# Sums of two quads in half-height products, with the last keys of all values between and behind them

## The chip, the cores and the metric

The kernel runs on one core of one Trainium2 chip. A core has five engines with queues of their own: TensorE (PE: matrix products, with its weight loads shown apart as PEld), VectorE (DVE), ScalarE (ACT), GpSimd (POOL) and SyncE (SP), which here only starts transfers. Products land in PSUM, eight banks of 128 partitions by 512 float32 numbers. The metric is the device time of one execution in microseconds (us), less is better; each number given for it is the median of several runs.

## What is computed

Cosine attention over 8 batches of 12 heads, 448 positions, 64 numbers a head, then a two-layer block with a leaky ReLU over all 3584 tokens.

```python
q_n = q / (np.linalg.norm(q, axis=-1, keepdims=True) + 1e-06)
k_n = k / (np.linalg.norm(k, axis=-1, keepdims=True) + 1e-06)
scores = np.matmul(q_n, k_n.transpose(0, 1, 3, 2)) / tau
attn = np.exp(scores - np.max(scores, axis=-1, keepdims=True))
attn = attn / (np.sum(attn, axis=-1, keepdims=True) + 1e-09)
x = np.matmul(attn, v)            # tokens x (12 heads * 64) = 3584 x 768
h = x @ w_in                      # 768 -> 2048
out = np.maximum(0.01 * h, h) @ w_out   # 2048 -> 768
```

The scores are bounded by 1/tau = 10, so the kernel takes the exponentials without the maximum.

## The kernel before

**Units.** A batch has 12 heads, that is six pairs (a *slot* s) and three quads of four heads (index j, three to a batch, `NQ = 3`). The 448 keys of a head are three tiles of 128 (`ki` = 0, 1, 2) and 64 *last keys*. Exponentials of scores lie in `pe[s]` (128 key rows, three tiles, two heads, 448 queries) and, for the last keys, in `pr[j]`: 128 rows, of which one half of 64 belongs to two heads of the quad and the other half to the other two. `rem_half(j, g)` says which half has head g of quad j; it changes over from one quad to the next. The values of the last keys lie likewise in `vrb`, with the other half of the rows zero, so that a product over all 128 rows takes only the right ones.

**Products of an attend.** For each quad the kernel needs the sums of the exponentials (weights: 32 columns of ones, so that each sum stands on 32 partitions) and, for the even and for the odd columns of v (`e` = 0, 1), the products with the values (32 columns each). One PSUM bank holds four strips of 32 partitions, one for each head. So a product here has 32 columns and goes to one strip: `strip_products` (L314) runs over key tiles and heads, four strips after each other; those over 128 rows are called `128*32` in the profile. `rem_products` (L301) does the last keys alone, over 64 rows (`64*32`), for two quads at once, whose heads use opposite halves of the rows.

**Order of an attend.** `attend_two` (L670) takes the first two quads of a batch: it deals banks (a pair for the sums, two pairs for the values), runs the last keys of sums and values by `rem_products`, then the sums of both quads with the reciprocals behind each (`totals`, `reciprocals`: ACT takes Ln of the bank at L339 and Exp of its negative at L340 into a tile `rb`), then the values of each quad (`products`) and their scaling by `rb` (`scale`, L361: DVE multiplies a PSUM bank by `rb` into `xT`, the transposed tokens). `attend` (L659) then takes the third quad by itself: four tiles of sums (the last through `ones_rem`, ones with half of the rows zero), four tiles of each half of the values. The first batch uses `attend` in another place, which does not change; seven batches go through `attend_batch` (L688).

**What stands around it.** After an attend, `firsts` runs the first layer for a chunk of tokens (L384: 16 blocks, each of six products over six slices of `xT`, the slices of quad j being 2j and 2j+1; the first three blocks are begun with four slices each). `visit` then runs the second layer of the chunk (L459, in halves of 64 rows), with key tiles of the next batch (L280 scores, L292 exponentials on ACT) dealt between. In both, `norm(s)` prepares later slots: `roots` (ACT, L200 and L201), `normalise` (DVE, L217, L218, L222), a transposing transfer on SP (L254), loads on SP, and a cast and squares on POOL.

**Order and banks.** The schedule is by hand: each engine runs its instructions in the order of the program text. `banks` deals the PSUM bank, or pair of banks, that was dealt or given back longest ago and isn't kept; a bank dealt with a name is kept until `given_back`. `behind` puts an empty instruction on an engine that waits for another one: on PE it is used where the other half of the rows goes on adding to the same bank.

Of the kernel before, what the change touches and what calls it, by code (L numbers as in the profile page):

```python
# [11 lines left out]
ALU = mybir.AluOpType  # L12
# [4 lines left out]
def kernel(  # L17
# [10 lines left out]
    nc = tc.nc  # L28
    B, H, S, D = q.shape
# [9 lines left out]
    NQ = NPAIR // 2  # L39
# [15 lines left out]
    qtp = ctx.enter_context(tc.tile_pool(name="qt", bufs=7))  # L55
    pep = ctx.enter_context(tc.tile_pool(name="pe", bufs=6))
    prp = ctx.enter_context(tc.tile_pool(name="pr", bufs=3))
    rbp = ctx.enter_context(tc.tile_pool(name="rb", bufs=2))
    xtp = ctx.enter_context(tc.tile_pool(name="xt", bufs=2))
    htp = ctx.enter_context(tc.tile_pool(name="ht", bufs=1))  # L60
    osp = ctx.enter_context(tc.tile_pool(name="os", bufs=3))
# [13 lines left out]
    def banks(count, keep=None, which=None):  # L75
        lo, hi = (0, 8) if not deals["apart"] else (0, 4) if count == 2 else (4, 8)
        x = which if which is not None else min(
            (i for i in range(lo, hi, count) if not set(range(i, i + count)) & set(sum(kept.values(), []))),
            key=lambda i: max(age[i : i + count]),
        )  # L80
        deals["n"] += 1
        age[x : x + count] = [deals["n"]] * count
        if keep:
            kept[keep] = list(range(x, x + count))
        return ps[:, x] if count == 1 else ps[:, x : x + count]

    def given_back(keep):
        deals["n"] += 1
        for i in kept.pop(keep):
            age[i] = deals["n"]  # L90
# [46 lines left out]
    def load_qk(s):  # L137
        if s >= NSLOT:
            return
        b, h0 = s // NPAIR, 2 * (s % NPAIR)  # L140
        both = raw_sb[:, s % NPAIR]
        nc.sync.dma_start(out=both[:, :, 0:3], in_=main(q, b, h0, 2))
        nc.sync.dma_start(out=both[:, :, 4:7], in_=main(k, b, h0, 2))
        for i, x in enumerate((q, k)):
            nc.sync.dma_start(
                out=both[64 * i : 64 * i + 64, :, 3],
                in_=x[b, h0 : h0 + 2, MAIN:S].rearrange("h p d -> p h d"),
            )
        raw[s] = (both[:, :, 0:4], both[:, :, 4:7])
# [3 lines left out]
    vb, vrb = {}, []  # L153
# [32 lines left out]
    def sums(s, parts=(0, 1)):  # L186
        if s >= NSLOT:
            return
        if s not in ss:
            ss[s] = smp.tile([128, 14], F32, name="ss")  # L190
        for i in parts:
            o = ss[s][:, 0:8] if i == 0 else ss[s][:, 8:14]
            nc.vector.tensor_reduce(  # L193
                o.rearrange("p (h t) -> p h t", h=2), sqs[s][i], axis=AX.X, op=ALU.add
            )
# [7 lines left out]
    qn, scalings = {}, {}  # L203

    def behind(eng, ins, why):

        tc.add_manual_dep(
            eng.nop().ins, ins.ins.name,
            mybir.DependencyInfo(mybir.DependencyClass.Sync, mybir.DependencyReason.DATA),
            reason=why,  # L210
        )
# [51 lines left out]
    pe, pr = {}, {}  # L263
# [30 lines left out]
    xT = {}  # L294

    rbs = {}

    def rem_half(j, g):
        return g // 2 ^ j % NQ % 2

    def rem_products(two, xs, weights):  # L301


        for g in range(4):
            for j, x in zip(two, xs):
                rows = slice(64 * rem_half(j, g), 64 * rem_half(j, g) + 64)
                nc.tensor.matmul(  # L307
                    out=x[32 * g : 32 * g + 32, :S],
                    lhsT=weights(j, g, rows),
                    rhs=pr[j][rows, g % 2, :],  # L310
                    start=True, stop=False,
                )

    def strip_products(j, x, weights, rem):  # L314

        begun = rem is None
        for ki in range(3 if begun else 4):
            for g in range(4):
                s, a = 2 * j + g // 2, g % 2
                nc.tensor.matmul(  # L320
                    out=x[32 * g : 32 * g + 32, :S],
                    lhsT=weights(g, ki) if ki < 3 else rem(g),
                    rhs=pe[s][:, ki, a, :] if ki < 3 else pr[j][:, a, :],
                    start=(ki == 0 and not begun), stop=(ki == (2 if begun else 3)),
                )

    sms = {}

    def totals(j, sm=None):
        rem = None if sm is not None else lambda g: ones_rem[:, rem_half(j, g)]  # L330
        sms[j] = banks(1) if sm is None else sm
        strip_products(j, sms[j], lambda g, ki: ones, rem)
        if sm is not None:
            reciprocals(j)

    def reciprocals(j):
        sm = sms.pop(j)
        rb = rbp.tile([128, S], F32, name="rb")
        nc.scalar.activation(rb, sm[:, :S], func=AF.Ln)  # L339
        nc.scalar.activation(rb, rb, func=AF.Exp, scale=-1.0)  # L340
        rbs[j] = rb

    pos = {}

    def products(j, e, po=None, begun=False):
        b, jj = divmod(j, NQ)
        if po is None:
            po = banks(1, (j, e))
        pos[j, e] = po
        vm = vb[j].rearrange("p h t (d e) -> p h t e d", e=2)  # L350
        vr = vrb[b % 2].rearrange("p j g (d e) -> p j g e d", e=2)
        strip_products(
            j, po, lambda g, ki: vm[:, g, ki, e], None if begun else lambda g: vr[:, jj, g, e]
        )

    def scale(j, e):
        b, jj = divmod(j, NQ)
        m, half = divmod(b, 2)
        if m not in xT:
            xT[m] = xtp.tile([128, KT, 2 * S], BF16, name="xT")  # L360
        scalings[j, e] = nc.vector.tensor_tensor(  # L361
            xT[m][:, 2 * jj + e, half * S : (half + 1) * S], pos.pop((j, e))[:, :S], rbs[j],
            op=ALU.mult,
        )
        if (j, e) in kept:
            given_back((j, e))

# [121 lines left out]
    ones = cpool.tile([128, 32], BF16, name="ones")  # L489
# [120 lines left out]
    roots(4)  # L610
    reciprocals(0)
    products(0, 0)

    scores(3, (0,))
    products(0, 1)
    scores(3, (1,))
    scaled(3)
# [4 lines left out]
    scores(3, (3,))  # L622
    fill(1)
    scale(0, 0)

    scores(4, (0,))
    fill(2)
    scores(4, (1,))
    totals(1)
    scaled(4)  # L630
    scale(0, 1)
    scores(4, (2,))
    transposes(5)
    reciprocals(1)
    products(1, 0)

    def begin(m, kts):
# [8 lines left out]
    for e in range(2):  # L646
        scale(1, e)
# [11 lines left out]
    def attend(j, behind=()):  # L659
        totals(j)  # L660
        reciprocals(j)
        po = banks(2)
        for e in range(2):
            products(j, e, po[:, e])
        for fn in behind:
            fn()
        for e in range(2):
            scale(j, e)

    def attend_two(j):  # L670
        two = (j, j + 1)
        sm = banks(2)
        po = [banks(2) for e in range(2)]
        vr = vrb[j // NQ % 2].rearrange("p j g (d e) -> p j g e d", e=2)
        rem_products(two, [sm[:, i] for i in range(2)], lambda j, g, rows: ones[rows])
        for e in range(2):
            rem_products(
                two, [po[e][:, i] for i in range(2)], lambda j, g, rows, e=e: vr[rows, j % NQ, g, e]
            )
        for i, j in enumerate(two):  # L680
            totals(j, sm[:, i])
        for i, j in enumerate(two):
            for e in range(2):
                products(j, e, po[e][:, i], True)
            for e in range(2):
                scale(j, e)

    def attend_batch(b):  # L688
        if b == 1:
            load_qk(14)  # L690
            load_qk(15)
            sums(12)
        attend_two(b * NQ)
        if b == 1:
            norm(12)
        attend(b * NQ + 2)


    def norm(s, transposed=True):
        if s >= NSLOT:  # L700
            return
        roots(s)
        normalise(s)
        if transposed:
            transposes(s)
        for x in (12, 13) if s == 11 else (s + 4,) if s > 11 else ():
            load_qk(x)
        ahead = {7: (), 8: (), 9: (10, 11), 10: (), 11: (12, 13)}.get(s, (s + 2,))
        if ahead:
            hold(qn[s][:, 6, 0, 0:1])  # L710
        for x in ahead:
            squares(x)
# [61 lines left out]
    for b in range(B):  # L774
# [16 lines left out]
        else:  # L791
# [3 lines left out]
            wide if b == 0 else four_late if b == 1 else three if tokens == 3 else four,  # L795
        )
        attend_batch(b + 1)
        for j in range((b + 2) * NQ, (b + 3) * NQ):
            load_v(j)
# [59 lines left out]
```

## Time and profile before

| what | us |
|---|---|
| runs of the kernel (median of 3; from, to) | 406.82 (406.67, 406.88) |
| the profiled execution, its own time | 406.75 |
| its span, first to last instruction | 404.9 |

| group of the profile | count | busy us | mean ns |
|---|---|---|---|
| L384, first layer | 760 | 147.4 | 352 |
| L459, second layer in halves of the rows | 1536 | 144.0 | 323 |
| L320, values, key tiles of 128 rows | 576 | 32.0 | 353 |
| L320, sums, key tiles of 128 rows | 288 | 16.7 | 354 |
| L320, last keys of values over 128 rows, half zeros | 80 | 7.3 | 352 |
| L320, last keys of sums over 128 rows, half zeros | 40 | 3.6 | 352 |
| L307, last keys of values over 64 rows | 112 | 4.0 | 350 |
| L307, last keys of sums over 64 rows | 56 | 2.7 | 360 |
| L361 on DVE, scaling | 48 | 27.7 | 619 |

The mean is the length of one instruction from its start to its modelled end. Products in different parts of the array overlap, so the busy time of a group is not count times mean, and the step from one to the next is shorter than the length. The share of PE is given by the union of its instructions. The granted clock of PE was 1.0 in the profiled execution.

### The profile page before, as it was taken

How to read it: one execution, taken by the hardware profiler on the slowest of the kernel's cores; microseconds unless marked ns; L12 is line 12 of the kernel's file. 1: busy time of each engine (PE TensorE's matmuls, PEld its weight loads, DVE VectorE, ACT ScalarE, POOL GpSimd, SP SyncE). 2: the span in 40 equal slices, each digit the busy share in tenths (PEclk: the TensorE clock that was granted, in tenths of full speed). 3: DMA queues.
4: the chain of work that ended last, by engine and by line, in shares of the span. 5: the costliest groups of instructions: out<-in, count | busy, mean ns of one | idle time of the engine just before them, and what ended most of it. 6: DMA issues, size and time to landing. Idle time of an engine off the chain costs nothing.

```text
span 404.9 us, 10159 instructions
## 1 busy us (share of the span) xinstructions
PE 397.6 (98%) x4086; PEld 225.4 (56%) x4096; DVE 188.1 (46%) x403; ACT 264.9 (65%) x458; POOL 140.1 (35%) x213
## 2 busy tenths in 40 slices
PE   8899999999999999999999999999999999999996
PEld 3335655444555555544886555544687555544564
DVE  6987723684655624454552626256361721130021
ACT  4997799556875689655876569745786559844200
POOL 4995533464344513343142513155122500000000
PEclk9999999999999999999999999999999999999999
DMA  7999999797789827576396844685386821110033
GB/s 188 249 226 244 214 186 219 181 183 179 157 190 153 148 62 180 117 129 170 76 181 141 126 117 120 157 117 138 90 174 120 95 45 40 40 41 2 0 78 79
DMA packets 100735, 54.21 MB, mean 134 GB/s; under 512 B 69424, under 2 KB 95440, under 8 KB 100688
## 3 DMA queue, kind: packets, MB, share of 16 engines
q1 hardware_dynamic: 76400, 40.13, 42.7%
q0 software_dynamic: 23440, 12.92, 23.5%
q8 instruction: 32, 0.52, 0.6%
q10 hardware_dynamic: 848, 0.52, 0.5%
q14 instruction: 15, 0.12, 0.1%
HBM read 45.61 MB, written 11.01 MB: 140 GB/s over the span
## 4 chain that ended last, share of the span: by engine, by line
PE 96%; ACT 1%; DVE 1%; issue 0%
PE ps L384 36%; PE ps L459 31%; PE ps L320 11%; PE ps L280 8%; PE ps L421 5%; PE ps L505 2%; PE ps L307 1%; ACT pe L292 1%; PE ps L236 1%; DVE qkT L261 0%; DVE qn L222 0%; ACT qkT L548 0%; ACT rb L340 0%; DVE warm L488 0%; DVE ss L193 0%
## 5 line engine op out<-in xcount | busy, mean ns | idle before, releaser
L384 PE MATMUL ps<-xT,w_in_sb 128*128 128x384 bf16 (+1 forms) x760 | 147.4, 352 | 0.4
L459 PE MATMUL ps<-w_out_sb,hT 64*128 64x384 bf16 x1536 | 144.0, 323 | 0.0
L292 ACT ACTIVATE pe<-ps 128x896 bf16<-128x896 f32 x144 | 124.4, 917 | 16.7 <-PE ps L280 14.9
L384 PEld LDWEIGHTS <-w_in_sb 128*128 128x128 bf16 x768 | 74.1, 98 | 71.5 <-issue 3.7
L391 ACT ACTIVATE hT<-ps 128x384 bf16<-128x384 f32 (+1 forms) x128 | 67.3, 543 | 67.2 <-PE ps L384 66.7
L459 PEld LDWEIGHTS <-hT 64*128 64x128 bf16 x1536 | 84.4, 94 | 44.7 <-PE ps L459 4.2
L182 POOL TENSOR_TENSOR sq<-raw_sb 128x512 f32<-128x512 f32 x90 | 82.7, 940 | 13.4 <-DMA raw_sb<-in_k_dram 12.6
L222 DVE TENSOR_TENSOR qn<-raw_sb,r 128x512 bf16<-128x512 f32 x96 | 56.8, 634 | 1.7
L280 PE MATMUL ps<-qkT 64*128 64x448 bf16 (+1 forms) x384 | 54.8, 353 | 1.6 <-DVE qkT L261 0.8
L193 DVE TENSOR_REDUCE ss<-sq 128x6 f32<-128x384 f32 (+1 forms) x95 | 54.5, 610 | 2.6 <-POOL sq L182 2.3
L471 DVE COPY osb<-ps 128x384 f32<-128x384 f32 x41 | 21.2, 553 | 69.7 <-PE ps L459 38.8
L514 POOL CAST seen<-qn 128x1 f32<-128x1 bf16 x44 | 8.2, 187 | 123.8 <-DVE qn L222 123.6
L217 DVE TENSOR_SCALAR ss<-ss 128x14 f32<-128x14 f32 x48 | 10.0, 209 | 73.9 <-ACT ss L201 73.8
L361 DVE TENSOR_TENSOR xT<-ps,rb 128x448 bf16<-128x448 f32 x48 | 27.7, 619 | 24.3 <-ACT rb L340 24.1
L160 POOL DMA_DIRECT2D v_b<-in_v_dram x24 | 18.6, 777 | 39.9 <-PE ps L320 39.9
L320 PE MATMUL ps<-pe,v_b 128*32 128x448 bf16 x576 | 32.0, 353 | 0.0
L280 PEld LDWEIGHTS <-qkT 64*128 64x128 bf16 (+1 forms) x384 | 17.8, 97 | 17.9 <-issue 6.6
L339 ACT ACTIVATE rb<-ps 128x448 f32<-128x448 f32 x24 | 12.9, 538 | 15.3 <-PE ps L320 14.3
L320 PEld LDWEIGHTS <-v_b 128*32 128x32 bf16 x576 | 15.1, 97 | 12.0 <-issue 0.6
L427 DVE COPY osb<-ps 128x384 f32<-128x384 f32 (+1 forms) x9 | 4.6, 513 | 36.6 <-issue 22.6
L421 PE MATMUL ps<-w_out_sb,hT 128*128 128x384 bf16 (+1 forms) x144 | 21.0, 308 | 0.0
L292 ACT ACTIVATE pr<-ps 128x896 bf16<-128x896 f32 x24 | 20.7, 923 | 0.2 <-PE ps L280 0.2
(52 smaller groups left out, 188.1 us busy)
## 6 DMA issues: line engine op xcount, KB each, us to landing
raw_sb<-in_q_dram SPq DMA_DIRECT2D x46, 192.0 KB, 3.3
raw_sb<-in_k_dram SPq DMA_DIRECT2D x44, 192.0 KB, 3.5
out_dram<-osb SPq DMA_DIRECT2D x30, 192.0 KB, 3.1
v_b<-in_v_dram POOLq DMA_DIRECT2D x24, 192.0 KB, 4.8
out_dram<-osb SPq DMA_DIRECT2D x12, 384.0 KB, 2.7
w_out_sb<-in_moe_w_out_dram POOLq DMA_DIRECT2D x4, 768.0 KB, 16.3
w_in_sb<-in_moe_w_in_dram POOLq DMA_DIRECT2D x3, 512.0 KB, 8.5
w_in_sb<-in_moe_w_in_dram POOLq DMA_DIRECT2D x2, 768.0 KB, 13.1
```

Of the source, the lines that this page charges most:

```text
L182: eng.tensor_tensor(sq, x, x, op=ALU.mult)
L193: nc.vector.tensor_reduce(o.rearrange("p (h t) -> p h t", h=2), sqs[s][i], axis=AX.X, op=ALU.add)
L222: scalings[s] = nc.vector.tensor_tensor(qn[s][:, lo:hi], x.rearrange("p h t d -> p t h d"), r[:, r0 : r0 + 2 * nt].rearrange("p (h t) -> p ...
L280: nc.tensor.matmul(out=out[:, a, :S], lhsT=x[rows, c0:c1], rhs=x[rows, 0:S], start=True, stop=True,)
L292: nc.scalar.activation(out=dst, in_=sc[:, :, :S], func=AF.Exp, scale=inv_tau)
L320: nc.tensor.matmul(out=x[32 * g : 32 * g + 32, :S], lhsT=weights(g, ki) if ki < 3 else rem(g), rhs=pe[s][:, ki, a, :] if ki < 3 else pr[j] ...
L361: scalings[j, e] = nc.vector.tensor_tensor(xT[m][:, 2 * jj + e, half * S : (half + 1) * S], pos.pop((j, e))[:, :S], rbs[j], op=ALU.mult,)
L384: nc.tensor.matmul(out=pm[:, :n], lhsT=w_in_sb[:, kt, m * 128 : (m + 1) * 128], rhs=xT[c // 2][:, kt, c0 : c0 + n], start=(kt == 0), stop= ...
L391: nc.scalar.activation(out=hT[c][:, m, :n], in_=pms.pop((c, m))[:, :n], func=AF.Prelu, alpha=0.01)
L421: nc.tensor.matmul(out=po2[:, :n], lhsT=hT[c][:, m, ts * 128 : (ts + 1) * 128], rhs=w_out_sb[:, m, lo : lo + n], start=(m == 0), stop=(m = ...
L459: done[p][i] = nc.tensor.matmul(out=pos2[p][:, i, :HALF], lhsT=hT[c][rows, m, ts * 128 : (ts + 1) * 128], rhs=w_out_sb[rows, m, half * HAL ...
L471: copy(out=osb[c, ts][:, half * HALF : (half + 1) * HALF], in_=po2[:, i, :HALF])
```

## The change

The two functions `attend_two` and `attend` give way, in the seven batches of `attend_batch`, to one, `attend_all`. It issues ten turns of eight `64*32` products (four strips times two halves of the rows). In them the lower half of the rows adds up the first quad's sums while the upper half adds up the second quad's; then each half does last keys of the four values of these quads (two turns); then each goes on with the other quad's sums; the tenth turn is the last keys of the third quad's values. For the two halves of the third quad's last keys to fill all eight places of that turn, its odd values stand with their pairs of heads changed over (strip c holds head c ^ 2), and the scaling puts them back: in two parts of 64 partitions, each read from the other half of the bank. Before a half goes on to the quad that the other half had begun, PE waits for the other half's last product there (`behind`, twice in an attend). Then come the first quad's even values, the third quad's sum, and the other values. Eight banks are dealt at once, six of them kept by name; there is a third `rb` buffer. In the second batch, `norm(12)` stands ahead of the attend instead of between its two parts.

```diff
-    rbp = ctx.enter_context(tc.tile_pool(name="rb", bufs=2))
+    rbp = ctx.enter_context(tc.tile_pool(name="rb", bufs=3))
...
-    def strip_products(j, x, weights, rem):
+    def strip_products(j, x, weights, rem, over=0):
...
-            for g in range(4):
+            for c in range(4):
+                g = c ^ over
                 s, a = 2 * j + g // 2, g % 2
                 nc.tensor.matmul(
-                    out=x[32 * g : 32 * g + 32, :S],
+                    out=x[32 * c : 32 * c + 32, :S],
...
-    def scale(j, e):
+    def scale(j, e, over=False):
...
-        scalings[j, e] = nc.vector.tensor_tensor(
-            xT[m][:, 2 * jj + e, half * S : (half + 1) * S], pos.pop((j, e))[:, :S], rbs[j],
-            op=ALU.mult,
-        )
+        po = pos.pop((j, e))
+        for lo, hi in ((0, 64), (64, 128)) if over else ((0, 128),):
+            p0 = lo ^ 64 if over else lo
+            scalings[j, e] = nc.vector.tensor_tensor(
+                xT[m][lo:hi, 2 * jj + e, half * S : (half + 1) * S],
+                po[p0 : p0 + hi - lo, :S], rbs[j][lo:hi], op=ALU.mult,
+            )
...
+    def attend_all(b):
+        j0 = b * NQ
+        sm = [banks(1) for i in range(2)]
+        po = {}
+        vr = vrb[b % 2].rearrange("p j g (d e) -> p j g e d", e=2)
+
+        def head(u, c):
+            return c ^ 2 if u == (2, 1) else c
+
+        def last_keys(u, v, c, h):
+            return u if rem_half(j0 + u[0], head(u, c)) == h else v
+
+        places = {}
+        for c in range(4):
+            for h in range(2):
+                x = [(h, None, ki) for ki in range(3)]
+                y = [(h ^ 1, None, ki) for ki in range(3)]
+                for z in (x, y):
+                    if rem_half(j0 + z[0][0], c) == h:
+                        z.append((z[0][0], None, 3))
+                mid = [last_keys((0, e), (1, e), c, h) + (3,) for e in range(2)]
+                places[c, h] = x + mid + y + [last_keys((2, 0), (2, 1), c, h) + (3,)]
+        seen, begun = {}, set()
+        for n in range(10):
+            turn = [(c, h) + places[c, h][n] for c in range(4) for h in range(2)]
+            waits = {}
+            for c, h, jj, e, ki in turn:
+                if e is None and (jj, c, h ^ 1) in seen and (jj, c, h) not in seen:
+                    waits[jj] = max(waits.get(jj, (-1,)), seen[jj, c, h ^ 1], key=lambda y: y[0])
+            for _, ins in waits.values():
+                behind(nc.tensor, ins, "the other rows' products in this bank")
+            for c, h, jj, e, ki in turn:
+                if e is not None and (jj, e) not in po:
+                    po[jj, e] = banks(1, (j0 + jj, e))
+            for i, (c, h, jj, e, ki) in enumerate(turn):
+                j, g = j0 + jj, head((jj, e), c)
+                rows = slice(64 * h, 64 * h + 64)
+                ins = nc.tensor.matmul(
+                    out=(sm[jj] if e is None else po[jj, e])[32 * c : 32 * c + 32, :S],
+                    lhsT=ones[rows] if e is None else vr[rows, jj, g, e],
+                    rhs=(pr[j] if ki == 3 else pe[2 * j + g // 2][:, ki])[rows, g % 2, :],
+                    start=(jj, e, c) not in begun, stop=e is None and h != jj and places[c, h][n + 1][1] is not None,
+                )
+                begun.add((jj, e, c))
+                if e is None:
+                    seen[jj, c, h] = (8 * n + i, ins)
+        for jj in range(2):
+            sms[j0 + jj] = sm[jj]
+            reciprocals(j0 + jj)
+
+        def values(jj, e):
+            products(j0 + jj, e, po[jj, e], True, head((jj, e), 0))
+            scale(j0 + jj, e, (jj, e) == (2, 1))
+
+        values(0, 0)
+        totals(j0 + 2)
+        reciprocals(j0 + 2)
+        for jj, e in ((0, 1), (1, 0), (1, 1), (2, 0), (2, 1)):
+            values(jj, e)
+
     def attend_batch(b):
         if b == 1:
             load_qk(14)
             load_qk(15)
             sums(12)
-        attend_two(b * NQ)
-        if b == 1:
             norm(12)
-        attend(b * NQ + 2)
+        attend_all(b)
```

More of the change, by code (lines that the diff above doesn't have):

```diff
@@ L343, with products @@
     pos = {}
-    def products(j, e, po=None, begun=False):
+    def products(j, e, po=None, begun=False, over=0):
         b, jj = divmod(j, NQ)
@@ L352, in products @@
         strip_products(
-            j, po, lambda g, ki: vm[:, g, ki, e], None if begun else lambda g: vr[:, jj, g, e]
+            j, po, lambda g, ki: vm[:, g, ki, e], None if begun else lambda g: vr[:, jj, g, e],
+            over,
         )
-    def scale(j, e):
+    def scale(j, e, over=False):
         b, jj = divmod(j, NQ)
@@ L668, in attend @@
             scale(j, e)
[L670 to L686, printed above, removed]
+    def attend_all(b):
[17 more added lines that the diff above has]
+                places[c, h] = x + mid + y + [last_keys((2, 0), (2, 1), c, h) + (3,)]
+        assert all(len(x) == 10 for x in places.values())
+        seen, begun = {}, set()
[33 more added lines that the diff above has]
+            values(jj, e)
```

## The prediction

> **What bounds the kernel now.** I read the page first: busy shares, then the chain that ended last.
>
> ```profile
> span 404.9 us, 10159 instructions
> PE 397.6 (98%) x4086; PEld 225.4 (56%) x4096; DVE 188.1 (46%) x403; ACT 264.9 (65%) x458; POOL 140.1 (35%) x213
> ...
> PE 96%; ACT 1%; DVE 1%; issue 0%
> ```
>
> TensorE (PE) is busy 98% of the span and is 96% of the chain; every other engine is at 65% or less. So a change pays or costs what it does to PE's own stream, as long as nobody makes PE wait. The list of who PE waited for confirms this: five entries, 3.2 us in all, none at the lines that the change touches, and asked for the stretch from 70 us on it is empty. PE has no slack there to hide work in either.
>
> The second view is the timeline of one attend (the stretch that turns the exponentials of one batch into sums and products), the one that begins at 216.74:
>
> ```profile
> 216.74 0.38 PE L307 MATMUL ps<-pr,ones 64*32 64x448 bf16 x8
> ...
> 216.94 0.56 PE L307 MATMUL ps<-pr,v_rem 64*32 64x448 bf16 x16
> ...
> 217.43 1.32 PE L320 MATMUL ps<-pe,ones 128*32 128x448 bf16 x24
> ...
> 218.57 2.44 PE L320 MATMUL ps<-pe,v_b 128*32 128x448 bf16 x48
> ...
> 220.84 0.74 PE L320 MATMUL ps<-pe,ones 128*32 128x448 bf16 x12
> 221.41 0.36 PE L320 MATMUL ps<-pr,ones_rem 128*32 128x448 bf16 x4
> ...
> 223.22 0.99 PE L384 MATMUL ps<-xT,w_in_sb 128*128 128x384 bf16 x5
> ```
>
> Columns: start, length, engine, line, operation, tiles, shape, count. A `128*32` product fills a quarter of the array's columns, so four run side by side; a `64*32` one fills an eighth, so eight do. I call one such set a turn. The 48 products of v_b, 12 turns, run from 218.57 to 220.84: 2.27 / 12 = **0.189 us a turn**. A narrow window gives the third turn of eight by itself:
>
> ```profile
> 217.12 0.37 PE L307 MATMUL ps<-pr,v_rem 64*32 64x448 bf16 x8
> ```
>
> So turns of eight step 216.74, 216.94, 217.12: 0.20 for the first, about 0.19 for the next, and then 0.31 to the first `128*32` product (217.43), since the shape changes. A turn of eight costs what a turn of four does and holds twice the products. The attend is 33 turns and lasts 6.48 us to the first L384. Taken by the same bounds, the seven attends last 6.57, 6.50 and five times 6.48.
>
> **The change part by part.**
>
> *Turns.* Before: 3 turns of eight (last keys of two quads' sums and values), then in fours: 6 for these quads' sums, 12 for their values, 4 for the third quad's sum, 8 for its values (2 of them on last keys, half of whose rows are zeros). After: the sums of two quads in halves are 2 x 4 x 3 x 2 = 48 products plus 8 on last keys, the values' last keys 6 x 4 = 24: 80 products, 10 turns of eight; then 4 turns for the third sum and 6 x 3 = 18 for values. 32 turns. PE issues 24 products and 24 weight loads more per attend, but in one turn less: **-0.189 us**, seven times: -1.32. There are as many changes of shape as before (0.31 into `128*32`, and the one into L384), so these cancel.
>
> *Two waits of PE on itself*, ahead of the sixth and the seventh turn of eight (n = 5 and n = 6), since the second half of the rows may add to a sum only when the first is out. Each waits for the last product of the turn three before. By the steps above that product starts 0.02 into its turn and lasts 0.36, so it ends 0.38 in, while the waiting turn is due at 3 x 0.19 = 0.57: the result is there in time. What is left is that the turn's weights aren't loaded ahead. The nearest row is the same wait behind two turns of L280:
>
> ```profile
> 119.18 0.35 PE L280 MATMUL ps<-qkT 64*128 64x448 bf16 x2
> 119.36 0.33 PE L459 MATMUL ps<-w_out_sb,hT 64*128 64x384 bf16 x2
> ```
>
> The weight loader shows 0.21 us idle there (released by PE), yet the step 119.18 to 119.36 is an ordinary 0.19. Lower bound: 0. Upper bound: a change of shape, where nothing is loaded ahead, 0.31 - 0.19 = 0.12. I take 0.02: there the 0.19 runs from the last product issued, and in a turn of eight the last is issued 0.02 after the first. 14 waits: +0.28 (0 to 1.7). Queued behind each wait are the remaining turns of PE alone.
>
> *First two attends.* They are 0.09 and 0.02 longer than the others. In the first, the second turn of L307 lasts 0.65 instead of 0.56 because a bank is still being copied out by DVE:
>
> ```profile
> 69.71 0.56 DVE L471 COPY osb<-ps 128x384 f32<-128x384 f32 x1 [5.47 <-PE ps L459]
> ...
> 70.05 0.65 PE L307 MATMUL ps<-pr,v_rem 64*32 64x448 bf16 x16
> ```
>
> The changed order asks for value banks only from the fourth turn on (some 0.58 in, 70.4, after the copy's end at 70.27). -0.11 for both; bounds -0.11 and 0.
>
> *The third sum's bank.* All eight banks are now taken, so the third sum reuses the first sum's, and waits for ACT's Ln of it. This Ln can start when the ninth turn's products end: 0.20 + 7 x 0.19 + 2 x 0.02 = 1.57 for the turn's start, 0.02 + 0.36 for its last product, 0.05 of signalling (L339 in the old order starts 0.05 after the product it needs) = 2.00. It takes 0.54 (218.23 in the timeline), so it ends at 2.54, some 2.6 with the signal back. The third sum is due after ten turns, the change of shape and three value turns: 1.76 + 0.31 + 0.20 + 0.19 + 0.19 = 2.65. Covered by 0.05 only. I take 0; the upper bound is 0.1 an attend (0.7 in all), if signals are slower, or where ACT is late, as in the first attend: roots(12) now stand ahead of the Ln (L200, L201, 0.29 + 0.21) and follow a reduction that ends at 71.33, so they end near 71.9, against 69.85 + 2.00 = 71.85.
>
> *Scalings.* The reciprocals come 0.5 us later than before (the Ln at 2.00 instead of 218.23 - 216.74 = 1.49). DVE then does six scalings at 0.54 each, and the last one in two halves of 64 rows, each as long as a whole one because the length is the 448 columns (618 ns median at L361): +0.62 us of DVE per attend. From 3.2, paced by the products, the two halves end near 7.7 after the start. L384 needs them for its sixth slice: it starts at 6.33, and twelve products of 0.163 (0.216 in the wider chunks) precede the fifth slice: 8.4 at the earliest. Hidden by 0.7 us, and what runs next on DVE (normalise, needed in the following visit) is later by as much. Cost 0; without cover, the whole 0.62 would show.
>
> *norm(12) moved* ahead of the second batch's attend: its roots (ACT), normalise (0.17 + 0.24 + 1.16 on DVE), one transposing DMA and one load on SP, the tiny cast and the squares on POOL. The two loads queued on SP ahead of it stay ahead. DVE's first scaling there moves from about 3.2 to 3.75 and has caught up by the third quad, since that one waits for products. 0. A third `rb` buffer only removes a wait of ACT on DVE.
>
> **Sum.** -1.32 + 0.28 - 0.11 = -1.15 us. Against the profiled execution (span 404.9, its time 406.75, so 1.85 around it): 405.60; it lay 0.07 below the median of 406.82, so against the median 405.67, say **405.7**.
>
> A rule bears on the sum. The Trainium skill (TensorE: Matmul & The Clock Gate, "Wait — 56ns, not 53.3ns?") has a floor of about 25 ns between starts of matmuls, however small, so that eight would need 200 ns, an estimate from that page; by it the ten turns would lose part of the gain (second rival). The trace disagrees so far: eight starts lie within 0.02 us, and the third turn follows at 0.19. The same source's TensorEngine Tiling (Array Packing), "Gotcha 1: PSUM Pressure", forbids two row halves the same bank at the same time; the turns of L307 already do this on different strips without a longer step.
>
> **The rivals.**
> 1. *The third sum waits for ACT* by 0.1 in each attend. For: cover is 0.05. Against: ACT is idle 0.9 us before its first Ln in the attend. 405.7 + 0.7 = 406.4.
> 2. *Turns of eight settle at 0.20.* For: the first step is 0.20. Against: that is also the first step after a change of shape in fours. Eight later steps x 0.011 x 7 = 0.62: 406.3.
> 3. *Each PE wait empties the array* and costs 0.10 instead of 0.02: 14 x 0.08 = 1.1: 406.8, no change. Against: the row at 119.36.
> 4. *Slower:* eight weight loads a turn stay hidden for three turns but not for ten, because they must be issued between products. It decides in turns 4 to 10. The gain of an attend, 0.189 - 0.04 + 0.016 = 0.165, is gone at 0.02 per step over eight steps. If one load (0.09, `64*32` loads at L307) stood open in each: 8 x 0.09 x 7 = 5.0: 410.7. For: only three turns in a row were ever seen. Against: the third showed no trace of it.
>
> That it does something else than it says I leave aside: the counts of products follow from the code.
>
> **How the numbers follow.** A difference under 0.2% (0.81 us) can't be told from none here. The forecast, with its own range of 405.3 (both waits free) to 406.0, has 0.67: faster. Rivals 1, 2 and 3 have 0.11, 0.07 and 0.05: within 0.2%. Rival 4 has 0.10: slower. So faster 0.67, same 0.23, slower 0.10. The range goes from 405.3 to 406.6, which takes in rivals 1 and 2.
>
> **What would show it.** Right: an attend of 6.3 us to its first L384; ten steps of about 0.19 at the new product line; PE's wait list without an entry for L320 on ACT or DVE. Wrong: a step over 0.22 at the two waits, a gap before the third sum's first product, L384 waiting for DVE L361, or steps of 0.20 and more through the turns of eight.

## The result, and the profile after

| | before | changed |
|---|---|---|
| median of 6 runs each, us | 406.85 | 405.43 |
| ratio, 95% interval | | 0.9963 (0.9951 to 0.9976) |
| profiled execution: its time, its span | 406.75, 404.9 | 405.48, 403.7 |

The changed kernel is faster: 1.42 us between the medians, 0.37% by the ratio, and no run of one kernel reaches into the runs of the other. The page's first lines and its chain look as before, a little shorter (columns: engine, busy time, share of the span, instructions; then shares of the chain by engine):

```profile
span 403.7 us, 10501 instructions
PE 396.3 (98%) x4254; PEld 224.7 (56%) x4264; DVE 194.5 (48%) x410; ACT 264.3 (65%) x458; POOL 139.5 (35%) x213
...
PE 96%; ACT 2%; DVE 1%; issue 0%
```

There are 168 products more on PE (24 in each of seven attends), yet PE is busy for less time. DVE has 6.4 us more, 4.3 of it the seven second halves of the last scalings, and PE does not wait for it: its list of waits has the same five entries as before, 3.2 us in all, and none of them lies behind 70 us. The same attend as before, in the timeline of the changed kernel:

```profile
216.25 0.76 PE L719 MATMUL ps<-pe,ones 64*32 64x448 bf16 x24
...
217.22 0.91 PE L719 MATMUL ps<-pe,ones 64*32 64x448 bf16 x24
...
217.97 0.37 PE L719 MATMUL ps<-pr,v_rem 64*32 64x448 bf16 x8
...
218.27 0.75 PE L321 MATMUL ps<-pe,v_b 128*32 128x448 bf16 x12
...
218.85 0.74 PE L321 MATMUL ps<-pe,ones 128*32 128x448 bf16 x12
...
222.55 1.64 PE L389 MATMUL ps<-xT,w_in_sb 128*128 128x384 bf16 x9
```

The tenth turn of eight starts at 217.97. Nine steps lie between 216.25 and that: 1.72, that is 0.20 and eight times 0.19. The attend ends at 222.55: 6.29 us. Its busy time by attend, from the view of windows (length, busy time of PE and count, then PEld):

```profile
70.04:76.33 6.29, 6.29 (x172) 3.34 (x169) 5.60 (x12) 4.74 (x10) 2.05 (x4) 1.00 0.63 189
122.28:128.58 6.29, 6.29 (x172) 3.39 (x169) 3.11 (x6) 4.67 (x10) 1.50 (x3) 1.00 0.74 148
164.09:170.38 6.29, 6.29 (x170) 3.35 (x169) 3.32 (x6) 4.03 (x9) 0.91 (x2) 1.00 0.20 75
```

All seven are 6.29 to 6.30 (starts to the nanosecond: 6.293 to 6.296), against 6.571, 6.503 and five times 6.48 before. The differences add up to 1.43 us. The stretches between the attends are the same within 0.001, and the tail too (45.39). What keeps the span's difference at 1.24 is the start: the first attend begins 0.19 later in this execution. In the other profiled kernels below it began anywhere from 69.78 to 70.31 (but where work was added at the start), so that is scatter ahead of the attends, not part of the change.

### The profile page after: what moved, and what is told of

The parts are those of the page before. It is cut to its first block, busy times and chain, and to the rows that moved or that the text cites. A ratio compares the mean times of both kernels' runs of the same rounds, so it can differ in the third digit from the quotient of the medians.

```text
span 403.7 us, 10501 instructions
## 1 busy us (share of the span) xinstructions
PE 396.3 (98%) x4254; PEld 224.7 (56%) x4264; DVE 194.5 (48%) x410; ACT 264.3 (65%) x458; POOL 139.5 (35%) x213
## 4 chain that ended last, share of the span: by engine, by line
PE 96%; ACT 2%; DVE 1%; issue 0%
PE ps L389 36%; PE ps L464 31%; PE ps L321 9%; PE ps L280 8%; PE ps L426 5%; PE ps L719 3%; PE ps L510 2%; ACT pe L292 1%; PE ps L236 1%; DVE qkT L261 0%; ACT qkT L553 0%; ACT pr L292 0%; ACT rb L341 0%; DVE warm L493 0%; ACT rb L340 0%
## 5 line engine op out<-in xcount | busy, mean ns | idle before, releaser
L222 DVE TENSOR_TENSOR qn<-raw_sb,r 128x512 bf16<-128x512 f32 x96 | 55.7, 621 | 1.7
L217 DVE TENSOR_SCALAR ss<-ss 128x14 f32<-128x14 f32 x48 | 11.5, 239 | 70.6 <-ACT ss L201 70.3
L366 DVE TENSOR_TENSOR xT<-ps,rb 128x448 bf16<-128x448 f32 (+1 forms) x55 | 33.3, 622 | 20.5 <-ACT rb L341 17.8
L321 PE MATMUL ps<-pe,v_b 128*32 128x448 bf16 x576 | 30.8, 353 | 0.0
L167 POOL DMA_DIRECT2D v_rem<-in_v_dram x32 | 19.8, 641 | 1.6 <-DMA w_out_sb<-in_moe_w_out_dram 1.6
```

The costliest lines, as they stand in the source:

```text
L222: scalings[s] = nc.vector.tensor_tensor(qn[s][:, lo:hi], x.rearrange("p h t d -> p t h d"), r[:, r0 : r0 + 2 * nt].rearrange("p (h t) -> p ...
L321: nc.tensor.matmul(out=x[32 * c : 32 * c + 32, :S], lhsT=weights(g, ki) if ki < 3 else rem(g), rhs=pe[s][:, ki, a, :] if ki < 3 else pr[j] ...
L366: scalings[j, e] = nc.vector.tensor_tensor(xT[m][lo:hi, 2 * jj + e, half * S : (half + 1) * S], po[p0 : p0 + hi - lo, :S], rbs[j][lo:hi], ...
```

## The experiments

**One part undone: the third quad's pairs in order again.** Its last keys of values then need two half-filled turns.

```diff
-            return c ^ 2 if u == (2, 1) else c
+            return c
...
-                places[c, h] = x + mid + y + [last_keys((2, 0), (2, 1), c, h) + (3,)]
...
+                mine = rem_half(j0 + 2, c) == h
+                places[c, h] = x + mid + y + ([(2, 0, 3), (2, 1, 3)] if mine else [])
...
-        for n in range(10):
...
+        for n in range(11):
...
-            scale(j0 + jj, e, (jj, e) == (2, 1))
+            scale(j0 + jj, e)
```

> The changed kernel with one part undone: the third quad's odd values stand in order again, so that its last keys take two half-filled turns of eight instead of one full one; 33 turns, and the last scaling is one piece again. Theory (a turn costs 0.19 us whether it is full or not, and the filled turn is the whole gain): attends of 6.48 us, that is 6.295 + 0.189, and a median of about 406.7 (405.43 + 7 x 0.189 = 406.75). Rival (the gain comes from summing in half-height products, or from the new dealing of banks): attends near 6.30 and a median near 405.4.

Measured: ratio to the kernel before 0.9997 (0.9988 to 1.0006), median 406.86 where the kernel before had 407.00 beside it; all seven attends 6.48. The timeline shows the eleventh turn: the eight v_rem products from 218.55 are two half-filled turns of four, the second 0.19 behind the first, and the change of shape follows 0.30 later.

```profile
218.37 0.36 PE L719 MATMUL ps<-pr,ones 64*32 64x448 bf16 x4
218.55 0.56 PE L719 MATMUL ps<-pr,v_rem 64*32 64x448 bf16 x8
219.04 0.37 PE L321 MATMUL ps<-pe,v_b 128*32 128x448 bf16 x4
```

A half-filled turn costs as much as a full one, and the sums in half-height products win nothing by themselves: seven turns of sums either way. The gain is the turn that the pair change fills. The first two attends were 6.48 here too, without their 0.09 and 0.02: these come from the order of the banks, not from the filled turn (in the kernel before, all but the first product of the third turn start late there, 0.05 behind the end of DVE's copy out of their bank).

**That turn alone, in the kernel before.** The third quad's last keys follow as a fourth turn of eight behind the three of `rem_products`.

```diff
+        third = banks(2, ("third", j + 2))
+        for c in range(4):
+            for e in range(2):
+                g = c ^ 2 * e
+                rows = slice(64 * rem_half(j + 2, g), 64 * rem_half(j + 2, g) + 64)
+                nc.tensor.matmul(
+                    out=third[32 * c : 32 * c + 32, e, :S],
+                    lhsT=vr[rows, (j + 2) % NQ, g, e],
+                    rhs=pr[j + 2][rows, g % 2, :],
+                    start=True, stop=False,
+                )
         for i, j in enumerate(two):
             totals(j, sm[:, i])
```

> The kernel before, with the filled turn alone: the third quad's last keys of values, odd ones with their pairs changed over, go as a fourth turn of eight behind the other three; sums stay whole products over 128 rows. 32 turns, as in the changed kernel. Theory (the turn gains 0.19 only where its operands and its bank are ready; at 0.58 us into the attend they aren't): in the third to the seventh attend the bank pair of the second layer's last rows, copied out until 0.72 us into the attend, holds the turn back by about 0.19, so these stay near 6.48; in the first two the exponentials of the third quad's last keys end 1.12 to 1.17 us into the attend, so these grow to about 6.9. Median about 407.6. Rival (32 turns are 32 turns wherever the filled one stands): attends of 6.30, but for the bank wait of 0.09 in the first, median 405.5.

Measured: ratio 1.0019 (1.0010 to 1.0028), median 407.70, slower. Attends: 6.90 twice, then 6.45 to 6.50. In the second attend (timeline):

```profile
123.36 0.92 ACT L292 ACTIVATE pr<-ps 128x896 bf16<-128x896 f32 x1
...
124.34 0.38 PE L690 MATMUL ps<-pr,v_rem 64*32 64x448 bf16 x8 [0.39 <-ACT pr L292]
```

The fourth turn waits for the exponentials of its keys, which end at 124.28. In the third attend it is its pair of banks:

```profile
165.72 0.48 ACT L476 COPY osb<-ps 128x384 f32<-128x384 f32 x1 [0.44 <-PE ps L464]
165.74 0.56 DVE L476 COPY osb<-ps 128x384 f32<-128x384 f32 x1 [5.17 <-ACT pe L292]
...
166.25 0.48 PE L690 MATMUL ps<-pr,v_rem 64*32 64x448 bf16 x8
```

The copies out of the two banks end at 166.20 (ACT) and 166.30 (DVE), and the eight products, usually out within 0.02 of each other (length 0.38 for the set), take 0.48: the first starts at 166.25 and the other seven from 166.35, 0.05 behind the one copy and 0.05 behind the other. So the same 32 turns win nothing where the filled one stands early. In the changed kernel the ten turns of eight put it 1.72 into the attend, by when both are long there; this is what the half-height sums do for the time. Whether the filled turn could stand late with the sums left whole, at the price of more changes of shape, was not run.

**The waits of PE on itself, with less cover.** First with both turns of last keys ahead of the sums, so that each wait is for the turn just issued (`places = mid + x + y + ...`), then with one turn ahead and one between (`mid[:1] + x + mid[1:] + y + ...`).

> The changed kernel with its two turns on last keys of the first two quads' values ahead of the sums instead of between their halves, so that each of the two waits is for the turn just issued. Theory (a wait is free only as long as its result, out 0.38 us after that turn began, is there when the weights are to be loaded): each waiting turn starts 0.38 plus a signal of 0.05 and a weight load of 0.09 behind the turn before, 0.5 to 0.6 instead of 0.19; attends of 6.29 + 2 x 0.36 = 7.0 us, span about 5 us longer (408.7). Rival (such a wait of PE on itself costs nothing, since PE writes in order anyway): 6.29 us, span 403.7. In the first two attends a bank may add some 0.07.

> The changed kernel with one turn of last keys ahead of the sums and one between their halves, so that each wait has one turn of cover instead of two. With none, the step to the waiting turn was 0.465 and 0.442 instead of 0.189. Theory (the waiting turn comes 0.465 behind the start of the turn it waits for, however many lie between): 0.465 - 0.189 = 0.276 for the first and about 0.25 for the second, attends of 6.295 + 0.15 = 6.45. Rival (any turn between hides the wait): 6.295.

Each was run once. Measured, with no turn between: steps of 0.465 and 0.442 to the two waiting turns, attends of 6.84 (third to seventh), span 407.8. The first two attends took 7.08 and 7.03, so the copies out of the banks added 0.24 and 0.20 there and not the 0.07 expected: the second turn starts only behind them, 0.37 and 0.35 into the attend. The weight loader shows where the time goes:

```profile
166.69 0.11 PEld L719 LDWEIGHTS <-ones 64*32 64x32 bf16 x8 [0.54 <-PE ps L719]
167.14 0.14 PEld L719 LDWEIGHTS <-ones 64*32 64x32 bf16 x16 [0.33 <-PE ps L719]
```

With one turn between: one step of 0.276, the second waiting turn after 0.200, attends of 6.39 to 6.40, span 404.3. So the waiting turn can start 0.465 after the start of the turn it waits for (0.189 + 0.276 is the same 0.465), not the 0.5 to 0.6 that I had put together; and when the first wait has moved everything back, the second is met. The changed kernel leaves 3 x 0.189 = 0.567, so 0.10 to spare. The theory held in kind; its size was too high by a third (0.36 a wait where 0.27 was measured), and for the second wait of the last kernel it was wrong.

**The third sum's bank without its cover.** `totals(j0 + 2)` and its reciprocals straight behind the ten turns.

> The changed kernel with the third quad's sum straight behind the ten turns of eight instead of behind the first quad's even values. Theory (the bank of the first sum is free only when ACT's Ln of it ends, 2.51 us into the attend, and the sum is due at 2.02): PE stands for about 0.55 us there, attends of 6.85, span 403.7 + 3.8 = 407.5; PE's list of waits names ACT L340. Rival (the cover of three value turns isn't needed): attends of 6.29, span 403.7.

Measured, in one run: attends of 6.84, span 407.6, and

```profile
PE ps L321 <- ACT rb L340: 3.3, 7, 0.5
...
219.91 0.54 ACT L340 ACTIVATE rb<-ps 128x448 f32<-128x448 f32 x1 [1.38 <-PE ps L719]
...
220.50 0.75 PE L321 MATMUL ps<-pe,ones 128*32 128x448 bf16 x12 [0.48 <-ACT rb L340]
```

(the first line from the list of who waited for whom: total, times, longest; the others from the timeline). The attend starts at 217.94, so the bank can be written 2.56 into it. In the changed kernel the third sum starts 218.85 - 216.25 = 2.60 in. The cover is 0.04.

**Two `rb` buffers instead of three.**

> The changed kernel with two rb buffers instead of three. Theory (ACT's Ln for the third sum then waits for the scaling of the first quad's odd values, to about 4.8 us into the attend instead of 4.07, and with it DVE's last scalings come later by up to 0.2 us, still ahead of the first layer's sixth slice): attends of 6.29, span 403.7 within 0.3. Rival (the third buffer is part of the gain): the first layer's products wait for DVE, span more than 404.5.

Measured, in one run: span 403.5, all attends 6.29 to 6.30. The third Ln starts 4.80 into the attend, as expected, and it hides. The third buffer is worth nothing that can be seen.

**All of the attend in half-height products.** Thirty-two turns of eight would save the change of shape inside the attend.

```diff
+        units = [(0, None), (1, None), (0, 0), (0, 1), (1, 0), (2, None), (1, 1), (2, 0), (2, 1)]
+        orders = [units, units[7:] + units[:7]]
...
-                    lhsT=ones[rows] if e is None else vr[rows, jj, g, e],
+                    lhsT=ones[rows] if e is None else vr[rows, jj, g, e] if ki == 3 else vm[jj][rows, g, ki, e],
```

> The changed kernel, with all of the attend in half-height products: sums and values of all nine units go in 32 turns of eight, the lower half of the rows through the units in order, the upper half two units behind, with a wait wherever a half goes on with what the other began; no change of shape inside the attend. Theory (turns of eight hold 0.189 for any length, and waits behind three turns cost nothing): the change of shape (0.305 where a turn would be 0.189) and the 0.200 behind it go, 0.127 an attend: 6.17 us each, median 405.43 - 0.89 = 404.5. Rival (twice the weight loads or 18 waits an attend begin to show over 32 turns, say 0.02 a turn): 6.8 us each, median 409.

Measured: ratio 1.0267 (1.0253 to 1.0281), median 417.84. Neither theory. Three attends are 6.18, just as expected, with every step behind the first 0.189 up to the first layer; the others are 7.64, 6.96, 6.60 and 7.25, each with one long stop, and the first layer waits besides:

```profile
PE ps L389 <- DVE xT L366: 8.1, 7, 1.3
PE ps L733 <- issue: 2.2, 3, 1.1
...
75.28 0.36 PE L733 MATMUL ps<-pe,v_b 64*32 64x448 bf16 x2
76.73 0.37 PE L733 MATMUL ps<-pe,v_b 64*32 64x448 bf16 x3 [1.09 <-issue]
```

The stop at 75.28 is in the middle of a turn, after two of its eight products, and its releaser is "issue": nothing that the profile shows. Counted in the program, the four stops stand at places 1730, 3011, 5570 and 9155 of PE's instruction stream. All are 194 or 195 more than a multiple of 256. Two more kernels ask whether that is the cause, and whether the late scalings can be mended:

> The kernel with all of the attend in half-height products, and 93 short products (186 instructions of PE, 16 columns each) more at its start, so that everything behind stands 186 places later in PE's instruction stream. In the unshifted one PE stood still four times, each time 194 or 195 places behind a multiple of 256 of that stream, 394 to 479 places into the first, second, fourth and seventh attend. Theory (instructions are fetched in blocks of 256, and a block is used up in 3.0 us by turns of eight, faster than the next one comes): the stops move to the same places of the stream, which now lie 478 places into the second attend, 393 into the fifth, perhaps 364 into the sixth, and 464 into the seventh; the first and the fourth attend, where no whole block is used up before place 293, run at 6.18 us. Rival (the stops belong to these attends, by a transfer or a buffer that is late there): they stay in the first, second, fourth and seventh.

> The kernel with all of the attend in half-height products, in another order: the upper half of the rows runs one unit and two turns behind the lower one, so that the values become complete three turns apart and not four within the last six turns. Theory (in the first order the last scalings came late together and held up the first layer by 8.1 us in all; the stops of PE inside the attends have another cause and stay, at places 409, 482 and 400 and perhaps 437 of the stream's blocks): the first layer's wait for DVE falls under 1 us, attends of 6.18 but for three or four stops of 0.3 to 1.3 us, median 407 to 408. Rival (the stops came from the late scalings too): 404.5, ahead of the changed kernel.

The first adds 93 short products at the start:

```diff
+    few = banks(1)
+    for i in range(93):
+        nc.tensor.matmul(
+            out=few[:, :16], lhsT=warm[:, :128], rhs=warm[:, :16], start=(i == 0), stop=(i == 92)
+        )
```

Measured, in one run (417.48): the stops are in the second attend (479 places in, a step of 1.05) and the fifth (393 in, 0.80), with a step of 0.24 in the seventh at 464 and nothing at 364; the first and fourth attends run at 6.21 and 6.18. All stops moved with the stream, to the same places of its blocks of 256. The second, in which the upper half of the rows runs through its units in another order, had its stops 438, 410 and 400 places into the first, second and seventh attend, again on block ends (a step of 0.215 in the fourth, 0.03 over the usual one, stands on one too); it had 417.76 as its median (ratio 1.0261, 1.0240 to 1.0283). Its undisturbed attends are 6.29 and not the expected 6.18: two of its waits have only one turn between, and the steps there are 0.23. And my other theory fell: the first layer waited 8.3 us for DVE, as much as before. In its fourth attend, which begins at 222.43, ACT takes the third quad's Ln only at 228.32, and DVE stands until its reciprocal is there at 229.5, while the first layer begins at 228.95. In the first order that Ln was as late (5.78 us into the attend; here 5.89; in the changed kernel 4.07). So it is the third sum that comes too late in both. An order that mends this was not tried, because the stops alone (two to four large ones an execution, which made their attends 0.4 to 1.5 longer) outweigh the 0.11 an attend that the shape change costs (6.29 against 6.18).

**The changed kernel again**, on the chip of the kernels without the pair change, with the fourth turn, and with all of the attend in half-height products.

> The changed kernel as it is, on the same chip as its variants. Both theories: attends of 6.29 to 6.30 us, median 405.4 within 0.3.

Measured: 405.58, ratio 0.9970 (0.9958 to 0.9981), attends 6.29 to 6.30.

## Why the prediction was right, step by step

- *Turns, -1.32:* right. The five undisturbed attends fell from 6.483 to 6.294, by 0.189. That it is the filled turn that pays was shown by undoing it alone.
- *Two waits, +0.28:* wrong in size; they cost nothing. The step that failed was "in a turn of eight the last is issued 0.02 after the first", from which I let the next turn start later. The trace of the changed kernel has all steps between turns of eight, behind the first, at 0.189 or 0.190 and the weights of the waiting turn loaded early enough:

```profile
217.11 0.10 PEld L719 LDWEIGHTS <-v_rem 64*32 64x32 bf16 x4 [0.16 <-PE ps L719]
217.12 0.59 PEld L719 LDWEIGHTS <-ones 64*32 64x32 bf16 x28
```

  The turn is due at 217.21, and its loads start at 217.11: 0.10 ahead, where a load takes 0.09. The lower bound of the prediction was the value. This is all of the difference between -1.15 forecast and -1.43 found in the attends.
- *First two attends, -0.11:* right, -0.089 and -0.018 beyond the turn.
- *The third sum's bank, 0 with a cover of 0.05:* right; the cover is 0.04, and 0.55 an attend shows without it.
- *Scalings, hidden by 0.7:* right. The last half ended at 224.08, 7.8 into the attend against 7.7 worked out; the first layer starts at 222.55 and reaches its sixth slice some 13 products of 0.163 later, at 224.67. 0.6 was left. (The page puts 0.37 of idle time of the weight loader ahead of the first layer down to "DVE xT L366", which the kernel before has as "issue". It is no wait for DVE: the same 0.37 stands there before and after, and PE's own list has no such entry.)
- *norm(12) and the third buffer, 0:* right; the first attend is as short as the others, and two buffers do as well.
- *Rivals.* Turns settling at 0.20: no, 0.189 in every one behind the first. This also answers the rule of a floor between starts (the Trainium skill, TensorE: Matmul & The Clock Gate, "Wait — 56ns, not 53.3ns?"): eight products start within 0.024 here, so no floor of 25 ns holds between products in different parts of the array. The third sum waiting and the emptied array: no. The slower one, that eight loads a turn can't be kept up, did not happen, neither in ten turns nor in 32, where the steps between the stops are 0.189 too. What failed in 32 was the supply of instructions at block ends of the stream, which I had not thought of.

## What to carry to other kernels

Where products take part of the array, count turns, not products: a turn of 448 columns cost 0.189 us here whether four or eight of its places were filled, so look for half-empty ones that can share. Then ask of the filled turn when its operands and its bank are there; the same turn gained 0.19 us in one place and nothing in another. A wait of PE on its own earlier result was free with two turns of other work between and cost up to 0.09 us with one; how much is enough can be measured by taking that work away.

## What the runs showed of the hardware that I had not expected

PE can use up its instructions faster than they come. In turns of eight it takes 16 instructions (a load and a product for each place) every 0.189 us, so 256 of them last 3.0 us. In three kernels made of nothing but such turns for 6.2 us, PE stood still nine times for 0.25 to 1.27 us beyond the usual step, each time 194 or 195 places behind a multiple of 256 of its stream; adding 186 instructions at the start moved the stops accordingly. The Trainium skill (Runtime: NRT & Kernel Launch, "Instruction fetch mechanics") says that instructions come in blocks of 256 through a queue of their own and that crossing into the next is mostly hidden. The size agrees: the page of the first of these kernels has

```profile
q8 instruction: 38, 0.62, 0.6%
```

that is 38 packets of 16 KB, and its 4852 loads and as many products make 38 blocks of 256. That the crossing stays hidden does not hold here: from one block end to the next took up to 4.45 us (from 72.28 to the end of the first stop at 76.73).

The trace has the time of each of these packets, and they account for the stops. The one of the first stop was moved from 74.39 to 75.27, and PE went on 1.46 later. All nine stops ended 1.2 to 1.5 us after a packet had landed, and that packet had started 1.0 to 2.3 us behind the end of the block before (ends of blocks counted at the weight loads). At the fast block ends without a stop (364 places into the sixth attend of the shifted kernel, for one) it had started at most 0.7 behind. By these times it is the late start of a packet that makes the stop; why some start late stays open.

The changed kernel's ten turns of eight use 160 instructions in 1.9 us, and the other 96 of a block, at 8 a turn, take 2.3 more: 4.2 at the least, less than the slowest block seen. It showed no stop in any attend of its two profiled executions, where each packet had landed 1.9 us or more before PE came to its block. A longer run of such turns would leave less than that; how much longer it may be was not tried.
